# A Mamba-2 scan and a SiLU block on one core: the loads of unit 2 move from ScalarE's queue to GpSimd's

## The chip, the cores and the metric

The kernel runs on one core of a Trainium2 chip. The metric is the device time of one execution in microseconds (us); smaller is better. The engines of the core run beside each other, each through its own list of instructions in a fixed order, and wait for one another by semaphores: TensorE (PE: matmuls; PEld: loading of weights), VectorE (DVE), ScalarE (ACT), GpSimd (POOL) and SyncE (SP, which here only issues transfers). Sixteen DMA engines move data between HBM and the on-chip memory. SP, ScalarE and GpSimd can each issue transfers; the issue is one instruction in that engine's list.

## The reference

The first half is a state-space scan over chunks of 32 tokens, the second an MLP with SiLU. Sizes: batch 4, 8 heads, 768 tokens, head size 32, state size 16; 3072 tokens by 256 for the MLP, with 2048 hidden columns.

```python
log_a = np.log(np.clip(a, 1e-06, 1.0))
for c in range(nc):                       # chunks of 32
    cum = np.cumsum(la, axis=-1)
    L = np.exp(cum[:, :, :, None] - cum[:, :, None, :]) * causal
    M = np.einsum('bhin,bhjn->bhij', Cc, Bc) * L
    y = np.einsum('bhij,bhjd->bhid', M, xc) + np.einsum('bhin,bhnd->bhid', Cc, state) * np.exp(cum)[..., None]
    Bx = np.einsum('bhjn,bhjd->bhjnd', Bc, xc) * np.exp(cum[:, :, -1:] - cum)[..., None, None]
    state = np.exp(la.sum(-1))[..., None, None] * state + Bx.sum(axis=2)
x = y.transpose(0, 2, 1, 3).reshape(3072, 256)
h = x @ w_in                              # 256 x 2048
out = (h / (1 + np.exp(-h))) @ w_out      # 2048 x 256
```

## The kernel before

**Tiling.** The tokens are cut into 12 units of 256 tokens (three for each of the four batches), and each unit into four chunks of 64. Two units make a pair, and the MLP works on a pair (512 tokens). Units 0 and 1 and the MLP of pair 0 are written out as a start-up script (L691 to L777) and the list `steps` (L836); from then on a loop `step(s)` interleaves the MLP of one pair with the scans of the next. The order of the instructions on every engine is that of the program text; no scheduler moves anything.

**A unit's scan.** `a` is clamped to 1e-6..1. Two DVE scans (`f_Ek`, `f_E1`) make the decay matrix E from the tile `ab`, one (`f_P`) makes the prefix products `pfx` from `pz`. `f_TP` transposes B and C of a unit on TensorE (L390); ScalarE copies them out (`bh`, `ct`) and scales C (`ce`). `f_B` multiplies B by the last column of E (`BT`). `f_G` (L437) and `f_D0` (L423) are the products on TensorE, `f_S` the state (DVE, `st`), `f_SM` two scalings of it on ScalarE (`sm`, L464), `f_C` gives `cw`, `f_M` multiplies in E, `f_Y` (L477, L486) makes the output and `f_X` copies it to `xf` on ScalarE. Units 0 and 1 take `ab` from a small matmul; from unit 2 on it is loaded from scratch tensors in HBM.

**Scratch tensors.** `a_first` holds the clamped `a` of batch 0 (unit 2 reads it). `a_in` (with a zero ahead of every chunk) and `a_zero` (first column zero) hold that of batches 1 to 3, from unit 3 on. They are made so: `f_A1` loads `a` into the tile `acl` (three loads on SP, L267), `f_A2` clamps it on DVE (L273) and writes it out by two transfers on SP (L274, L275); `f_A0` writes the zero columns from GpSimd's queue (L283). `load_ab(3)` and `load_pa(3)` read them back.

**Weights.** They come as 64-bit numbers in 16 tiles `raw` of 512 KB (0 to 7 of `w_in`, 8 to 15 of `w_out`), all loaded on SP. For each, `w_size` runs two ScalarE operations (L188, L191), `w_bits` three on DVE (L202 to L205) and one or two on GpSimd (L207), and the fp32 tile w is ready. In the start-up, `f_s1(u, j)` (L526, eight matmuls) multiplies unit u's `xf` by weight tile j, with a SiLU on ScalarE after it (`gT`, L529); `f_s2` (L539) is the second matrix. `raw` has six buffers (pool `quad`).

**Loads of the first units.** ScalarE's queue issues B of unit 0 (L248), C of unit 2 (L743) and B of unit 2 (L752), each as two transfers of 64 KB in pieces of 64 bytes. GpSimd's queue issues B and C of unit 1, half of x of unit 1, x of unit 2 and B of unit 3, SP's all else. In the compiled program every transfer that SP or ScalarE issues takes one of eight completion semaphores, and its issue waits until the earlier transfer with that semaphore has landed. GpSimd's have eight of their own.

The script around the change, before (cut):

```python
    f_Ek(1, 0)
    load_n(2, 1, nc.scalar)
    ...
    f_s1(0, 2)
    w_bits(3, 2)
    w_size(4)
    f_A0()
    load_n(2, 0, nc.scalar)
    ...
    f_SM(1)
```

Of the kernel before, what the change touches and what calls it, by code (L numbers as in the profile page):

```python
# [8 lines left out]
FP32 = mybir.dt.float32  # L9
# [4 lines left out]
ALU = mybir.AluOpType  # L14
# [19 lines left out]
def kernel(  # L34
# [22 lines left out]
    nc = tc.nc  # L57

    batch, H, S, D = x.shape
    N = B.shape[-1]  # L60
    Q = 64
# [9 lines left out]
    loads = ctx.enter_context(tc.tile_pool(name="loads", bufs=1))  # L71
# [14 lines left out]
    def block(name, dtype=FP32):  # L86

        return blk.tile([128, 512], dtype, name=name, tag="blk", bufs=NB)
# [20 lines left out]
    def load_ab(u, q):  # L109
        ab[u] = loads.tile([128, 2, H, Q], FP32, name="ab")  # L110
        src, n = (a_first, 4 * u) if u < UPB else (a_zero, 4 * u - NC0)
        for c in range(2):
            q.dma_start(out=ab[u][64 * c:64 * c + 64].rearrange("p k h t -> p k (h t)"),
                        in_=src[n + c:n + 4:2].rearrange("(o k) h t -> o k (h t)", o=1).to_broadcast([64, 2, H * Q]))

    def load_n(u, i, q):
        b, t0 = at(u)
        if i == 0:
            t = bn[u] = (block("bn0")[:, 0:256].rearrange("p (k h n) -> p k h n", k=2, h=H) if u in (0, 1, 3) else
                         loads.tile([128, 2, H, N], FP32, name="bn"))  # L120
        else:
            t = tbc[u] = block("tbc0")[:, 0:256].rearrange("p (k h n) -> p k h n", k=2, h=H)
        for k in range(2):
            q.dma_start(out=t[:, k], in_=(B, C)[i][b, :, t0 + 128 * k:t0 + 128 * k + 128].rearrange("h p n -> p h n"))

    def load_t(u, i, q):
        b, t0 = at(u)
# [16 lines left out]
    def load_bcx(u, what="bcx"):  # L144
        if "c" in what:
            if 0 < u < UPB:
                load_n(u, 1, nc.sync)
            else:
                load_t(u, 0, nc.sync)
                load_t(u, 1, nc.sync)  # L150
        if "b" in what:
            load_n(u, 0, nc.sync)
        if "x" in what:
            load_x(u, nc.sync)
# [19 lines left out]
    def load_w(n, q):  # L174
        j = n % 8
        src = wi[:, :, j * WF:(j + 1) * WF] if n < 8 else wo[:, 2 * j:2 * j + 2]
        if src.dtype == FP32:
            w32[n] = block("w32")
            q.dma_start(out=two(w32[n]), in_=src)
            return  # L180
        t = raw[n] = quad.tile([128, 2, WF, 2], U32, name="raw", tag="quad")
        q.dma_start(out=t.rearrange("p k f two -> p k (f two)"), in_=src.bitcast(U32))

    def w_size(n, what="uv"):
        if n in raw:
            if "u" in what:
                u = wu[n] = block("wu")
                nc.scalar.activation(two(u), raw[n][:, :, :, 1].bitcast(FP32), AF.Abs)  # L188
            if "v" in what:
                v = wv[n] = block("wv")  # L190
                nc.scalar.activation(two(v), raw[n][:, :, :, 0], AF.Copy, scale=2.0 ** -51, bias=2.0)  # L191

    def w_bits(n, parts=1):
        if n in raw:
            u, v, hi = two(wu.pop(n)), two(wv.pop(n)).bitcast(U32), raw[n][:, :, :, 1]
            w32[n] = block("w32")
            for i in range(parts):
                fs = slice(WF // parts * i, WF // parts * (i + 1))
                if i == 0 or n == 0:
                    ws = fs if n == 0 else slice(0, WF)  # L200
                    ui = u[:, :, ws].bitcast(U32)
                    nc.vector.tensor_scalar(out=u[:, :, ws], in0=u[:, :, ws], scalar1=LEAST, scalar2=MOST,  # L202
                                            op0=ALU.max, op1=ALU.min)
                    nc.vector.tensor_scalar(out=ui, in0=ui, scalar1=3, scalar2=None, op0=ALU.logical_shift_left)
                    nc.vector.scalar_tensor_tensor(out=v[:, :, ws], in0=hi[:, :, ws], scalar=0x80000000, in1=v[:, :, ws],  # L205
                                                   op0=ALU.bitwise_and, op1=ALU.bitwise_or)
                nc.gpsimd.tensor_tensor(out=two(w32[n])[:, :, fs].bitcast(U32), in0=u[:, :, fs].bitcast(U32),  # L207
                                        in1=v[:, :, fs], op=ALU.add)
# [23 lines left out]
    NC1 = NC0 * (batch - 1)  # L232
# [34 lines left out]
            nc.sync.dma_start(out=acl[NC0 * (b - 1):NC0 * b],  # L267
                              in_=bass.AP(tensor=a.tensor, offset=a.offset + b * H * S, ap=[[Q, NC0], [S, H], [1, Q]]))

    def f_A2():  # L270

        r = slice(0, NC1)
        nc.vector.tensor_scalar(out=acl[r], in0=acl[r], scalar1=1.0, scalar2=1e-6, op0=ALU.min, op1=ALU.max)  # L273
        nc.sync.dma_start(out=a_in[:, :, 1:].rearrange("h c t -> c h t"), in_=acl[r])  # L274
        nc.sync.dma_start(out=a_zero[:, :, 1:], in_=acl[r, :, 1:])  # L275

    misc = block("misc")
    idle = misc[:, 0:UT].bitcast(BF16)
    nc.vector.memset(idle, 0.0)

    def f_A0():
        for t in (a_in[:, :, 0:1].rearrange("h c t -> c h t"), a_zero[:, :, 0:1]):
            nc.gpsimd.dma_start(out=t, in_=misc[:NC1, 0:H].rearrange("p (h t) -> p h t", t=1))  # L283

    warm = nc.const_aps.tensor(1.0, [128, 512], BF16)

# [50 lines left out]
    def f_P0(u, engine):  # L337
        src = pa[u].rearrange("p (c t) -> p c t", t=Q)
        PZ[u] = (pz, pz1, pz)[u]
        engine.tensor_scalar(out=PZ[u][:, :, 1:], in0=src, scalar1=1.0, scalar2=1e-6, op0=ALU.min, op1=ALU.max)  # L340
# [32 lines left out]
    def f_B(u, engine=nc.vector, ks=slice(0, 2)):  # L373
        if u not in BT:
            BT[u] = sc.tile([128, 2, H, N], FP32, name="BT")
        engine.tensor_tensor(out=BT[u][:, ks], in0=bn[u][:, ks],
                             in1=E[u][:, ks, :, Q - 1:Q].to_broadcast([128, ks.stop - ks.start, H, N]), op=ALU.mult)
# [144 lines left out]
    def f_s1(u, j):  # L522
        hp = two(half("hp"))
        for i in range(2):
            for kc in range(KC):
                nc.tensor.matmul(out=hp[:, i], lhsT=two(w32[j])[:, kc, 128 * i:128 * i + 128],  # L526
                                 rhs=two(XF[u])[:, kc], start=(kc == 0), stop=(kc == KC - 1))
        GT[u, j] = block("gT")
        nc.scalar.activation(two(GT[u, j]), hp, AF.Silu)  # L529
        if j == 7:  # L530
            XF.pop(u)
# [169 lines left out]
    f_A1()  # L701
    load_a(2)
    load_w(4, nc.sync)
    load_ab(2, nc.sync)
    load_w(5, nc.sync)
    f_Ab(0, 1, slice(4, 8))
    f_Ek(0, 0, slice(4, 8))
    f_Ek(0, 1, slice(0, 4))
# [22 lines left out]
    busy(2)  # L731
    f_X(0)
    w_bits(1, 2)
    w_size(2)
    f_s1(0, 0)
    w_size(3)
    w_bits(2, 2)
    f_s1(0, 1)
    f_TP(1)
    for e in range(2):  # L740
        f_T2(1, e)
    f_Ek(1, 0)
    load_n(2, 1, nc.scalar)  # L743
    for n in range(6, 8):
        load_w(n, nc.sync)
    f_Ek(1, 1)
    f_B(1, nc.gpsimd)
    f_s1(0, 2)
    w_bits(3, 2)
    w_size(4)  # L750
    f_A0()
    load_n(2, 0, nc.scalar)  # L752
    for n in range(8, 10):
        load_w(n, nc.sync)
    load_bcx(3, "c")
    f_G(1)
    f_D0(1)
    w_bits(4, 2)
    f_P(1)
    f_C(1, nc.gpsimd)  # L760
    f_P0(2, nc.gpsimd)
    load_x(2, nc.gpsimd)
    f_S(1)
    f_SM(1)
    f_M(1, 0)
# [5 lines left out]
    f_X(1)  # L771
    w_size(6)
    w_bits(5)
    f_A2()
    load_pa(3, nc.sync)
    load_w(10, nc.sync)
    load_n(3, 0, nc.gpsimd)  # L777

    def stage(u, what):
        for c in what:  # L780
            if c == "L":
                load_unit(u)
            elif c == "a":
                load_ab(u + 1, nc.sync)
            elif c == "x":
                load_x(u, nc.sync)
            elif c == "T":
                if 0 < u < UPB:
                    f_TP(u)
                else:  # L790
                    f_T(u, 0)
                    f_T(u, 1)
                f_T2(u, 0)
                f_T2(u, 1)
            elif c == "P":
                f_P(u)
            elif c in "12":
                f_E1(u, int(c) - 1, 2)
            elif c == "B":
                f_B(u)  # L800
            elif c == "C":
                f_C(u)
            elif c == "D":
                f_G(u)
                f_D0(u)
            elif c == "M":
                f_M(u, 0)
                f_M(u, 1)
            elif c == "S":
                f_S(u)  # L810
            elif c == "s":
                f_SM(u)
            elif c == "Y":
                f_Y(u)
                f_X(u)
            elif c == "h":
                f_xh(u)
            elif c == "l":
                f_xl(u)
            elif c == "d":  # L820
                f_xd(u)
# [4 lines left out]
    def todo(text):  # L826

        for step in text.split():
            if ":" in step:
# [3 lines left out]
            n = int(step[1:].split(".")[0])  # L833
            {"b": w_bits, "s": w_size, "h": w_h, "l": w_l, "d": w_d, "v": partial(w_d, vector=True), "m": f_s2, "p": s1_d, "r": load_r}[step[0]](n)

    steps = ((1, 0, "2:PT1"), (1, 1, "2:C2Ba"), (1, 2, "3:x b6 r11 s7"), (1, 3, "2:DSsM r12"),  # L836
             (1, 4, "b7 r13 s8"), (0, 5, "3:T s9"), (1, 5, "2:Y b8 r14"), (0, 6, "3:1PC s10"),
             (1, 6, "b9 r15 3:2B s11 h0 l0"), (0, 7, "2:h s12"), (1, 7, "3:D b10 3:SsM"))
    for u, j, text in steps:
# [119 lines left out]
```

## Time and profile before

| | us |
|---|---|
| median of 3 runs | 339.09 (338.19 to 339.94) |
| the profiled execution | 338.53 |
| its span, first to last instruction | 336.8 |
| TensorE busy | 323.6 (96%) |
| VectorE busy | 249.3 (74%) |
| ScalarE busy | 220.8 (66%) |
| GpSimd busy | 87.8 (26%) |

Mean granted TensorE clock: 0.989. The busy times are of one execution, taken by the hardware profiler. Waiting and the issuing of transfers are not counted as busy. In the page's slices each digit is the busy share of a fortieth of the span, in tenths. In a chain of waits each line is a piece of work or waiting that the next one needed.

### The profile page before, as it was taken

The numbers are of one execution on the slowest core, as the hardware profiler recorded it, in microseconds if no ns is written. First come the engines' busy times: TensorE is split into PE (matmuls) and PEld (weight loads), VectorE is DVE, ScalarE is ACT, GpSimd is POOL, SyncE is SP. The second block draws the span as 40 slices with busy tenths as digits, with TensorE's granted clock in tenths as the row PEclk, the third lists the DMA queues.
The fourth block names the chain that finished last, engine by engine and source line by source line (L and its number), as shares of the span: only waits on it lengthen the run. The fifth ranks groups of instructions, "written<-read, shape, count | busy, mean of one in ns | idle before, by whom it ended". The sixth has DMA issues, their size and how long they took to land.

```text
span 336.8 us, 7981 instructions
## 1 busy us (share of the span) xinstructions
PE 323.6 (96%) x3219; PEld 262.1 (78%) x3221; DVE 249.3 (74%) x414; ACT 220.8 (66%) x422; POOL 87.8 (26%) x89
## 2 busy tenths in 40 slices
PE   8883999999999999999999999999999999999995
PEld 5552788888878778878778778788778788899995
DVE  7964579987778798998866897965996873484443
ACT  3652568676568998857685766676666756656661
POOL 6865524557310212122102231202231202000000
PEclk9999699999999999999999999999999999999999
DMA  6999475777876394263340164420153000012001
GB/s 136 284 271 271 120 199 172 183 129 137 160 141 109 83 170 83 55 115 64 77 84 0 47 111 71 110 45 0 49 110 64 2 2 0 0 25 40 0 2 62
DMA packets 85732, 31.87 MB, mean 95 GB/s; under 512 B 69364, under 2 KB 76276, under 8 KB 85696
## 3 DMA queue, kind: packets, MB, share of 16 engines
q1 hardware_dynamic: 75888, 24.68, 31.9%
q0 software_dynamic: 3280, 6.03, 9.7%
q10 hardware_dynamic: 6528, 0.66, 1.5%
q8 instruction: 25, 0.41, 0.5%
q14 instruction: 11, 0.09, 0.1%
HBM read 22.79 MB, written 3.32 MB: 78 GB/s over the span
## 4 chain that ended last, share of the span: by engine, by line
PE 90%; DVE 4%; DMA 3%; issue 1%; ACT 0%; DVEq 0%
PE hp L562 23%; PE hp L554 11%; PE oa L603 9%; PE oa L604 9%; PE b L634 9%; PE oa L539 8%; PE hp L526 6%; PE gy L486 3%; PE b L629 2%; PE b L612 2%; PE oa L612 2%; PE gy L477 2%; DMA raw<-in_moe_w_in_dram 2%; PE gy L437 2%; PE gy L423 1%; DVE E L352 1%
## 5 line engine op out<-in xcount | busy, mean ns | idle before, releaser
L556 ACT ACTIVATE hp<-hp 128x512 f32<-128x512 f32 x80 | 46.6, 582 | 70.6 <-PE hp L554 70.5
L576 DVE TENSOR_TENSOR gl<-g,gh 128x512 fp32r<-128x512 f32 x62 | 42.8, 690 | 50.4 <-ACT gh L572 47.5
L562 PE MATMUL hp<-xh,wh 128*128 128x512 f32 x160 | 65.4, 409 | 0.0
L580 DVE SCALAR_TENSOR_TENSOR gd<-gh,g 128x512 fp32r<-128x512 f32 x80 | 59.5, 747 | 5.2 <-ACT gh L572 5.2
L562 PE MATMUL hp<-xl,wl 128*128 128x512 f32 x160 | 62.7, 392 | 0.0
L576 POOL TENSOR_TENSOR gl<-g,gh 128x512 fp32r<-128x512 f32 x18 | 29.3, 1629 | 121.5 <-ACT gh L572 121.5
L572 ACT ACTIVATE gh<-g 128x512 fp32r<-128x512 f32 x80 | 50.6, 632 | 2.7
L603 PE MATMUL oa<-gh,wh 128*128 128x512 f32 x128 | 50.0, 390 | 0.0
L604 PE MATMUL oa<-gl,wl 128*128 128x512 f32 x128 | 49.9, 390 | 0.0
L554 PE MATMUL hp<-xd,wd 128*128 128x512 f32 x160 | 49.6, 391 | 0.0
L570 ACT ACTIVATE g<-hp 128x512 f32<-128x512 f32 x80 | 47.5, 594 | 0.6 <-PE hp L562 0.6
L562 PEld LDWEIGHTS hp<-xh,wh 128*128 128x128 f32 x160 | 30.1, 188 | 8.8 <-ACT hp L556 2.6
L526 PE MATMUL hp<-xf,w 128*128 128x256 f32 x128 | 31.9, 402 | 4.5 <-POOL w L207 3.9
L554 PEld LDWEIGHTS hp<-xd,wd 128*128 128x128 f32 x160 | 30.0, 188 | 6.6
L634 PE MATMUL b<-gd,wd 128*128 128x512 f32 x128 | 34.5, 389 | 0.0
L562 PEld LDWEIGHTS hp<-xl,wl 128*128 128x128 f32 x160 | 30.1, 188 | 4.8
L207 POOL TENSOR_TENSOR w<-wu,wv 128x512 uint32<-128x512 uint32 (+1 forms) x21 | 26.1, 1250 | 25.3 <-DVE wv L205 25.3
L526 PEld LDWEIGHTS hp<-xf,w 128*128 128x128 f32 x128 | 24.5, 199 | 10.0 <-POOL w L207 5.8
L352 DVE TENSOR_TENSOR_SCAN E<-ab,diag 128x512 f32<-128x512 f32 (+1 forms) x26 | 29.1, 1150 | 1.3 <-PE ab L359 0.8
L539 PE MATMUL oa<-gT,w 128*128 128x256 f32 x128 | 28.8, 381 | 0.0
L603 PEld LDWEIGHTS oa<-gh,wh 128*128 128x128 f32 x128 | 24.0, 188 | 5.1
L604 PEld LDWEIGHTS oa<-gl,wl 128*128 128x128 f32 x128 | 24.0, 188 | 5.1
(105 smaller groups left out, 468.2 us busy)
## 6 DMA issues: line engine op xcount, KB each, us to landing
ab<-a_zero SPq DMA_DIRECT2D x18, 256.0 KB
raw<-in_moe_w_in_dram SPq DMA_DIRECT2D x8, 512.0 KB
raw<-in_moe_w_out_dram SPq DMA_DIRECT2D x8, 512.0 KB
wl<-w POOLq DMA_DIRECT2D x16, 256.0 KB, 4.0
xt<-in_x_dram SPq DMA_DIRECT2D x21, 128.0 KB
out_dram<-ot SPq DMA_DIRECT2D x40, 64.0 KB
tbc<-in_C_dram SPq DMA_DIRECT2D x40, 32.0 KB
pz<-a_in SPq DMA_DIRECT2D x9, 130.0 KB
```

The source lines that it names most:

```text
L526: nc.tensor.matmul(out=hp[:, i], lhsT=two(w32[j])[:, kc, 128 * i:128 * i + 128], rhs=two(XF[u])[:, kc], start=(kc == 0), stop=(kc == KC - 1))
L539: nc.tensor.matmul(out=OA[0][m][:, UT * u:UT * u + UT], lhsT=two(w32[8 + j])[:, i, 128 * m:128 * m + 128], rhs=two(GT[u, j])[:, i], start= ...
L554: nc.tensor.matmul(out=HP[s], lhsT=two(WD[f // 2])[:, kc, 128 * (f % 2):128 * (f % 2) + 128], rhs=XD[P][:, kc], start=(kc == 0), stop=Fals ...
L556: nc.scalar.activation(HP[s], HP[s], AF.Copy, scale=HALF / UP)
L562: nc.tensor.matmul(out=HP[s], lhsT=two(w[f // 2])[:, kc, 128 * (f % 2):128 * (f % 2) + 128], rhs=x_[P][:, kc], start=False, stop=(kc == KC ...
L570: nc.scalar.activation(G[s], HP.pop(s), AF.Silu, scale=UP)
L572: nc.scalar.activation(GH[s], G[s], AF.Copy, scale=DOWN)
L576: engine.tensor_tensor(out=GL[s], in0=G[s], in1=GH[s].bitcast(FP32), op=ALU.subtract)
L580: nc.vector.scalar_tensor_tensor(out=GD[s], in0=GH[s].bitcast(FP32), scalar=1.0 + 1.0 / HALF, in1=G.pop(s), op0=ALU.mult, op1=ALU.subtract)
L603: nc.tensor.matmul(out=OA[P][m], lhsT=two(WH[n])[:, r, ms], rhs=gh, start=(f == 0), stop=False)
L604: nc.tensor.matmul(out=OA[P][m], lhsT=two(WL[n])[:, r, ms], rhs=gl, start=False, stop=(f == NF - 1))
L634: nc.tensor.matmul(out=B2[P][:, m], lhsT=two(WD[n])[:, r, 128 * m:128 * m + 128], rhs=gd, start=(fresh and s == tiles[0]), stop=True, skip ...
```

## The change

ScalarE issues only B of unit 0 (two transfers). C of unit 2 goes to GpSimd's queue in two halves, with w3 between them, B of unit 2 and x of unit 3 as whole loads. The clamp of `acl` moves from DVE to GpSimd and is done twice: in place, after w1 (`f_A2(True)`), and once more into a block of its own `acz`, with its first column set to zero, after w2 (`f_A2(False)`). The writes to the scratch tensors become `f_A3`, three transfers on SP right after raw tile 7: the zero column of `a_in`, `a_in`, and all of `a_zero`. On SP, raw 5 goes ahead of `ab` of unit 2; C and B of unit 3 and `pz` of unit 3 ahead of raw 8 and 9; raw 10 behind `ab` of unit 3.

```diff
-    def load_n(u, i, q):
+    def load_n(u, i, q, ks=(0, 1)):
         b, t0 = at(u)
-        if i == 0:
-            t = bn[u] = (block("bn0")[:, 0:256].rearrange("p (k h n) -> p k h n", k=2, h=H) if u in (0, 1, 3) else
-                         loads.tile([128, 2, H, N], FP32, name="bn"))
-        else:
-            t = tbc[u] = block("tbc0")[:, 0:256].rearrange("p (k h n) -> p k h n", k=2, h=H)
-        for k in range(2):
-            q.dma_start(out=t[:, k], in_=(B, C)[i][b, :, t0 + 128 * k:t0 + 128 * k + 128].rearrange("h p n -> p h n"))
+        if i == 1:
+            if u not in tbc:
+                tbc[u] = block("tbc0")[:, 0:256].rearrange("p (k h n) -> p k h n", k=2, h=H)
+        elif u not in bn:
+            bn[u] = (block("bn0")[:, 0:256].rearrange("p (k h n) -> p k h n", k=2, h=H) if u in (0, 1, 3) else
+                     loads.tile([128, 2, H, N], FP32, name="bn"))
+        for k in ks:
+            q.dma_start(out=(bn, tbc)[i][u][:, k], in_=(B, C)[i][b, :, t0 + 128 * k:t0 + 128 * k + 128].rearrange("h p n -> p h n"))
...
-    def f_A2():
+    acz = block("acz").rearrange("p (h t) -> p h t", t=Q)
+
+    def f_A2(first):
 
         r = slice(0, NC1)
-        nc.vector.tensor_scalar(out=acl[r], in0=acl[r], scalar1=1.0, scalar2=1e-6, op0=ALU.min, op1=ALU.max)
+        nc.gpsimd.tensor_scalar(out=(acl if first else acz)[r], in0=acl[r], scalar1=1.0, scalar2=1e-6, op0=ALU.min, op1=ALU.max)
+        if not first:
+            nc.gpsimd.memset(acz[r, :, 0:1], 0.0)
+
+    def f_A3():
+
+        r = slice(0, NC1)
+        nc.sync.dma_start(out=a_in[:, :, 0:1].rearrange("h c t -> c h t"), in_=misc[r, 0:H].rearrange("p (h t) -> p h t", t=1))
         nc.sync.dma_start(out=a_in[:, :, 1:].rearrange("h c t -> c h t"), in_=acl[r])
-        nc.sync.dma_start(out=a_zero[:, :, 1:], in_=acl[r, :, 1:])
+        nc.sync.dma_start(out=a_zero, in_=acz[r])
...
-    def f_A0():
-        for t in (a_in[:, :, 0:1].rearrange("h c t -> c h t"), a_zero[:, :, 0:1]):
-            nc.gpsimd.dma_start(out=t, in_=misc[:NC1, 0:H].rearrange("p (h t) -> p h t", t=1))
...
     load_w(4, nc.sync)
+    load_w(5, nc.sync)
     load_ab(2, nc.sync)
-    load_w(5, nc.sync)
...
     w_bits(1, 2)
+    f_A2(True)
     w_size(2)
     f_s1(0, 0)
     w_size(3)
     w_bits(2, 2)
+    f_A2(False)
     f_s1(0, 1)
     f_TP(1)
     for e in range(2):
         f_T2(1, e)
     f_Ek(1, 0)
-    load_n(2, 1, nc.scalar)
     for n in range(6, 8):
         load_w(n, nc.sync)
     f_Ek(1, 1)
     f_B(1, nc.gpsimd)
+    load_n(2, 1, nc.gpsimd, (0,))
     f_s1(0, 2)
     w_bits(3, 2)
     w_size(4)
-    f_A0()
-    load_n(2, 0, nc.scalar)
-    for n in range(8, 10):
-        load_w(n, nc.sync)
-    load_bcx(3, "c")
+    load_n(2, 1, nc.gpsimd, (1,))
+    f_A3()
     f_G(1)
     f_D0(1)
     w_bits(4, 2)
     f_P(1)
     f_C(1, nc.gpsimd)
     f_P0(2, nc.gpsimd)
+    load_n(2, 0, nc.gpsimd)
     load_x(2, nc.gpsimd)
+    load_bcx(3, "c")
+    load_pa(3, nc.sync)
     f_S(1)
     f_SM(1)
...
     w_bits(5)
-    f_A2()
-    load_pa(3, nc.sync)
-    load_w(10, nc.sync)
+    for n in range(8, 10):
+        load_w(n, nc.sync)
     load_n(3, 0, nc.gpsimd)
...
             elif c == "x":
-                load_x(u, nc.sync)
+                load_x(u, nc.gpsimd)
...
-    steps = ((1, 0, "2:PT1"), (1, 1, "2:C2Ba"), (1, 2, "3:x b6 r11 s7"), (1, 3, "2:DSsM r12"),
+    steps = ((1, 0, "2:PT1"), (1, 1, "2:C2Ba r10"), (1, 2, "3:x b6 r11 s7"), (1, 3, "2:DSsM r12"),
```

## The prediction

> **What bounds the kernel now.** I read the page's slices first, then the chain of waits in order of time, then the engines' timelines and a table of stretches around the place that the chain pointed to.
>
> ```profile
> PE   8883999999999999999999999999999999999995
> PEclk9999699999999999999999999999999999999999
> DMA  6999475777876394263340164420153000012001
> ```
>
> One slice is 8.42 us. From slice 5 on (33.7 us) TensorE is busy all the time, at full clock from slice 6 on: a wait on another engine after about 40 us costs nothing, and whatever brings TensorE to that point earlier should move the end by the same amount. The only hole is slice 4 (25 to 34 us, busy 3 tenths), and slice 5 is the only one with a low clock. Here is the chain of waits across it (start, length, what):
>
> ```profile
> 21.34 6.79 DMA raw<-in_moe_w_in_dram
> 28.13 0.02 issue
> 28.16 3.59 DMA bn<-in_B_dram
> 31.74 0.02 issue
> 31.77 0.70 ACT sm L464 x2
> ...
> 32.56 1.08 PE gy L477 x32
> 33.64 1.13 PE gy L486 x61
> ...
> 35.23 3.78 PE hp L526 x8
> 39.01 0.75 PE gy L390 x4
> 39.75 5.18 PE hp L526 x24
> ```
>
> A 128-column scaling on ScalarE (sm) waits for a load that it does not read. The timeline of ScalarE says why:
>
> ```profile
> 20.47 2.37 ACTq L124 DMA_DIRECT2D tbc<-in_C_dram  x2
> 22.88 0.60 ACT L529 ACTIVATE gT<-hp 128x512 f32<-128x512 f32 x1 [2.34 <-DMA ab<-a_first]
> 28.16 3.56 ACTq L124 DMA_DIRECT2D bn<-in_B_dram  x2
> 31.77 0.69 ACT L464 ACTIVATE sm<-st,par 128x128 f32<-128x128 f32 x2 [7.17 <-DMA bn<-in_B_dram]
> ```
>
> ScalarE issues C and B of unit 2 itself. One issue takes 0.375 us (the view of L124), but in the compiled order each waits until an older transfer on the same completion semaphore has landed: B's first for raw tile 7 (28.13), its second for a later one. So ScalarE stands for 2.34 and 7.17 us. DVE had written st by 27.50 (its row at 26.27 lasts 1.23), so sm could have run then. TensorE meanwhile:
>
> ```profile
> 28.70:32.50 3.80, 0.03 (x1) 0.00 (x0) 0.00 (x0) 0.73 (x3) 1.73 (x2) 1.00 1.06 240
> 32.50:34.80 2.30, 2.19 (x96) 1.86 (x96) 1.24 (x3) 2.07 (x5) 0.00 (x0) 0.54 0.48 80
> 36.00:39.50 3.50, 3.50 (x12) 2.77 (x11) 1.07 (x1) 1.01 (x2) 3.50 (x3) 0.50 0.36 74
> ```
>
> Columns: stretch, length, busy PE, PEld, DVE, ACT, POOL, clock, DMA share, GB/s. After 3.8 us without matmuls the clock is half for about 7 us. The gap costs twice: 3.8 us of waiting, and about 7 x 0.5 = 3.4 us of slow matmuls.
>
> **What the Trainium skill says.** "DMA: Bandwidth & Descriptors", section Anatomy of one DMA: the DMA engines do not wait on semaphores, the wait is on the issuing sequencer before dispatch. The trace agrees: two issues of 0.375 us hold ScalarE for 3.56. The same page, Issuing engines are not separate DMA queues: loads from any engine run on the same 16 DMA engines, so moving the issue saves only the issuer's time. The DMA share of 1.06 at 28.7 to 32.5 fits: no bandwidth is gained. "TensorE: Matmul & The Clock Gate", section What's actually happening: one idle window of about 3.4 us halves the clock; the 3.8 us gap agrees. "GPSIMD Engine Reference", Specifications: GpSimd shares SBUF interfaces with VectorE; L207 on 128x512 took 3.03 us at 35.10 against 1.26 at 44.43, which fits.
>
> **The change part by part**, as a re-timing of 15 to 40 us on the times of this trace. Names: w3 is weight tile 3; s1(u,j), G, D0, Y, TP are TensorE's blocks of unit u.
>
> *GpSimd gains two clamps and a memset.* In the new order A2(True) stands between w1 and w2 on GpSimd, and it waits for the three loads of acl. They were issued at 12.61 to 14.06 on SP right behind a_first, and a_first landed just before 17.80, when SP's load of ab that waits for it goes. I take 18.5 for acl. GpSimd's rows now:
>
> ```profile
> 17.75 1.42 POOL L207 TENSOR_TENSOR w<-wu,wv 128x256 uint32<-128x256 uint32 x2 [0.63 <-DVE wv L205]
> 20.05 0.68 POOL L376 TENSOR_TENSOR BT<-bn,E 128x256 f32<-128x256 f32 x1 [0.89 <-issue]
> 21.69 1.41 POOL L207 TENSOR_TENSOR w<-wu,wv 128x256 uint32<-128x256 uint32 x2 [0.96 <-DVE wv L205]
> 25.64 1.72 POOL L207 TENSOR_TENSOR w<-wu,wv 128x256 uint32<-128x256 uint32 x2 [0.92 <-DVE wv L205]
> ```
>
> A clamp of 256 columns costs 0.39 (L340), and L207 goes from 0.71 to 1.26 when its columns double, so a clamp of 512 is about 0.7. The queue: clamp 18.55 to 19.25; w2 (1.42) to 20.7, so 1.5 later; second clamp and memset to 21.6; BT 22.3 (was 20.73); first half of C(2), 0.92 as the loads of GpSimd show, to 23.3; w3 to 24.7 (was 23.1); second half of C(2) to 25.6; w4 to 27.1 (was 27.36); cw 0.7 and the clamp of pz 0.4 to 28.2; B(2), two issues, 28.25 to 30.1; x(2) to 32. Bounds of a clamp: 0.4 and, if it is stretched like the slow L207 (x 2.4), 1.7.
>
> *ScalarE loses four issues.* TensorE starts s1(0,2) on the first half of w2 at 20.1 and ends at 22.05 (was 20.5). So gT is at 22.1, the two halves of w_size(4) at 22.6 and 23.2: 0.77 earlier than now, although 2.34 of waiting went; the delay of w2 eats the rest. DVE: w4's bits to 24.8 (was 25.55), pfx 0.7, st 1.2, ending 26.7; M to 27.95. sm follows st at 26.7 to 27.4, against 31.77.
>
> *TensorE.* G and D0 of unit 1 at 22.1 to 23.2, s1(0,3) 24.0 to 26.0 (was 22.47), s1(0,4) 26.4 to 28.4, then Y(1): sm, M and cw are all there, so it starts at 28.4 instead of 32.56. At full clock it takes 1.4 (as in the later Y rows, 0.62 + 0.79), xf 0.45: s1(1,0) runs 30.3 to 32.1, where it ended at 39.01. Up to here 6.9 us are gained, and no gap of TensorE is longer than about 1.3 us, so the low clock should not come.
>
> *What is late next: B(2).* TP(2) is the next block, and it reads it. Now B(2) was in long before 39.01; in the new order its second issue starts on GpSimd at 29.2. GpSimd's loads of B took 4.3 (issued at 38 to 40, queue nearly empty) and 7.8 (issued at 6 to 9, queue full) from issue to landing; x(2), issued at 28.55, took 4.0. In the new order raw 8 and 9 stand behind unit 3's B, C and pz on SP, so the load is light there; I take 4.3. B(2) lands at 33.5, three transposes more: TP(2) ends at 33.95 instead of 39.75, of which TensorE idles 1.4. Gain: 5.8 us.
>
> *The rest*, at nothing. C(2) is issued at 22.35 and 24.7 and even at 7.8 us lands at 32.5, before B(2). raw 8 and 9 land some 3 us later, at about 34; ScalarE reads raw 8 at 48.37 now, about 42.5 then. raw 10 moves from 38.05 to behind ab(3), which waits for DVE's second scan (42.52 now, 37.1 then), and its raw tile is read after 55 now. x(3) from GpSimd adds 1.9 us of issue ahead of w6; GpSimd is free from 33.3, w6's input comes from DVE at 38.5, and TensorE needs w6 only after Y(2). If this cover were gone, w6 would be late by at most these 1.9 us. DVE's clamp (0.41 at 34.93) was no wait. The write of a's zero column goes from GpSimd to SP, which has nothing urgent then. pz(3) is earlier than before. After 40 us the order of the other engines hangs on TP(2), since DVE's cw waits 3.87 for ScalarE's ce behind it, so they move up with it.
>
> Sum: the profiled execution took 338.53 (span 336.8 and 1.7 around it); minus 5.8 is 332.7. The median shown is 339.09, 0.56 above. I forecast 333.0.
>
> **The rivals.**
> *GpSimd becomes the bound.* For: two clamps, a wait and eight more issues in its queue, and L207 at 3.03 us once. Against: it is busy 7.22 of the 10 us from 10 to 20 and 3.71 of the next 5, so 4 of 15 us are free. Clamps of 1.7 put w4, cw and B(2) 2.0 later: TP(2) at 35.95, gain 3.8; with acl another 1 us later 2.8. About 335.2.
> *The new wait replaces the old one.* B(2) is late and TensorE idles so long that the clock drops again. With a landing at about 35.5 the gap from 32.1 is 3.4, the loss of clock 3.4, and TensorE is at 35.95 + 3.4 = 39.35 where it is 39.75 now: about 338.4, no change. For: 7.1 to 7.8 us for GpSimd's 64 KB loads when queues were full (1.06 DMA share at 28.7). Against: 4.0 for x(2) in that very stretch.
> *Slower: the same load, as slow as the slowest here.* GpSimd 1 us late, so issued at 30.2, 7.8 to land: 38.0, TP(2) to 38.45, a gap of 5.9 and 3.4 of half clock: 41.85 against 39.75, 2.1 lost, 340.6. It decides from a landing at 35.9 on (35.9 + 0.45 + 3.4 = 39.75), 6.7 us after an issue at 29.2.
>
> **How the numbers follow.** Forecast 333.0: 0.66, its own range 331.3 (B(2) not late at all: TP(2) would end at 32.55, gain 7.2) to 334.8. GpSimd bound: 0.14. Wait replaced: 0.08. Slower: 0.12. The range reaches into the second case: 331.3 to 336.8. Half a per cent is 1.7 us, about what a measurement of this kernel tells from no change. Faster 0.80 (the first two), same 0.08, slower 0.12.
>
> **What would show it.** In the new profile: no ACTq row after the first two; sm at about 27; w2 on GpSimd at about 19.3 behind the clamp; Y(1) at about 28.4 and slice 5 of PEclk at full; a PE wait for B(2) of 1 to 2 us before L396 and s1(1,1) at about 34. The forecast is wrong if that wait is over 3 us or brings a half clock, if acl lands well after 18.5, or if TensorE shows new holes after 40 us, with raw 8 to 10 or w6 as the releaser.

## The result and the profile after

The median of 20 runs is 335.96 us (333.86 to 340.54), that of the kernel before, 20 runs beside them, 339.90 (338.19 to 340.98). The ratio is 0.9882, 95% interval 0.9857 to 0.9908: the change saves 3.9 us of the 6.1 that were forecast (333.0 against 339.09). The ratio is that of the means without the runs more than 1.5% above a kernel's fastest (five of these twenty, 338.93 to 340.54 us, and two each in x2_later and three_raws below); with all twenty it is 0.9912. The other fifteen still spread from 333.86 to 338.48, where the kernel before spreads over 2.8 us. They sort by TensorE's mean clock: seven with 0.998 or more lie at 333.86 to 336.00, seven with 0.993 to 0.995 at 334.86 to 338.48, one with 0.988 at 338.17; the five left out have 0.990 to 0.995, no less than these. (Half clock for 3.4 us, as in the profiled execution, takes 0.005 off the mean: 0.5 x 3.4 / 336.7.) The profiled execution took 338.48 us, the slowest of the fifteen, and so shows what goes wrong. The page's slices:

```profile
PE   8868699999999999999999999999999999999996
PEclk9999799999999999999999999999999999999999
DMA  6997685777886394263440163430163000012001
```

The hole of slice 4 is filled, from 3 to 8 tenths. But slice 3 fell from 8 to 6, slice 5 from 9 to 6, and slice 5 kept a low clock (7 tenths, before 6). TensorE's timeline (start, length, line, out<-in, shapes, count, idle time ahead and what ended it; the lines of the changed kernel that are quoted here are numbered 1 to 6 higher from L116 on):

```profile
29.59 0.69 PE L483 MATMUL gy<-cw,sm 32*64 32x64 f32 x32
...
31.55 1.99 PE L532 MATMUL hp<-xf,w 128*128 128x256 f32 x8 [0.47 <-ACT xf L502]
33.97 0.30 PE L396 MATMUL gy<-ident,bn 128*128 128x128 f32 x1 [0.43 <-DMA bn<-in_B_dram]
37.30 0.33 PE L396 MATMUL gy<-ident,bn 128*128 128x128 f32 x1 [3.03 <-DMA bn<-in_B_dram]
...
37.82 6.89 PE L532 MATMUL hp<-xf,w 128*128 128x256 f32 x24
```

Y(1) starts at 29.59 instead of 32.56 and s1(1,0) ends at 33.5 instead of 39.0. Then TP(2) waits 0.43 us for the first half of B of unit 2 and 3.03 for the second. The chain of waits runs through the same place:

```profile
28.85 0.40 POOL pz L346
29.25 0.06 issue
29.31 0.94 POOL bn L125
30.25 0.00 issue
30.25 7.00 DMA bn<-in_B_dram
37.26 0.04 issue
37.30 0.73 PE gy L396 x3
38.03 6.68 PE hp L532 x24
44.71 0.62 PE gy L443 x32
```

GpSimd has issued the second half at 30.25, and it lands 7.00 us later. The 24 matmuls after it take 6.68 us; at full clock they take 5.3 (5.38 for the next 24). The table of stretches (stretch, length, busy PE, PEld, DVE, ACT, POOL, clock, DMA share, GB/s) shows the gap and the clock after it:

```profile
34.00:37.20 3.20, 0.27 (x1) 0.08 (x1) 1.27 (x1) 0.17 (x1) 3.20 (x5) 1.00 1.05 305
37.50:40.90 3.40, 3.40 (x11) 2.77 (x10) 1.65 (x3) 1.11 (x3) 0.13 (x1) 0.50 0.43 84
```

By 44.71 this execution is only 0.23 us ahead of the kernel before (44.94), and it ends as early as that one (338.48 against 338.53). The gain of 3.9 us is presumably that of executions in which this second gap costs less; none of them was profiled.

What went out beside B? SP's timeline and GpSimd's, in this order:

```profile
29.30 0.62 SPq L106 DMA_DIRECT2D pz<-a_in  x1
30.02 0.93 SPq L183 DMA_DIRECT2D raw<-in_moe_w_out_dram  x2
```

```profile
18.97 0.61 POOL L276 TENSOR_SCALAR acl<-acl 36x512 f32<-36x512 f32 x1 [1.03 <-DMA acl<-in_a_dram]
19.66 1.41 POOL L208 TENSOR_TENSOR w<-wu,wv 128x256 uint32<-128x256 uint32 x2
...
29.31 1.83 POOL L125 DMA_DIRECT2D bn<-in_B_dram  x2
31.13 1.76 POOL L143 DMA_DIRECT2D xt<-in_x_dram  x2
```

SP issued raw 8 and 9, 1 MB, 0.2 us before the second half of B, and x of unit 2 stood right behind it on GpSimd. Either could be what held it up. The clamp waited 1.03 us for acl, and w2 behind it.

### The profile page after: what moved, and what is told of

It reads as the page before. It is cut to its first block, busy times and chain, and to the rows that moved or that the text cites. A ratio compares the mean times of both kernels' runs of the same rounds, so it can differ in the third digit from the quotient of the medians.

```text
span 336.7 us, 7984 instructions
## 1 busy us (share of the span) xinstructions
PE 324.1 (96%) x3219; PEld 261.5 (78%) x3221; DVE 253.2 (75%) x413; ACT 221.1 (66%) x422; POOL 91.6 (27%) x96
## 4 chain that ended last, share of the span: by engine, by line
PE 90%; DMA 8%; POOL 1%; SPq 0%; DVE 0%; issue 0%
PE hp L568 23%; PE hp L560 11%; PE oa L609 9%; PE oa L610 9%; PE b L640 9%; PE oa L545 8%; PE hp L532 6%; DMA a_first<-ach 3%; PE gy L492 2%; PE b L635 2%; PE b L618 2%; PE oa L618 2%; PE gy L443 2%; DMA bn<-in_B_dram 2%; DMA ab<-a_first 2%; PE gy L483 2%
## 5 line engine op out<-in xcount | busy, mean ns | idle before, releaser
L582 POOL TENSOR_TENSOR gl<-g,gh 128x512 fp32r<-128x512 f32 x18 | 29.2, 1621 | 121.9 <-ACT gh L578 121.9
L358 DVE TENSOR_TENSOR_SCAN E<-ab,diag 128x512 f32<-128x512 f32 (+1 forms) x26 | 30.9, 1213 | 1.7 <-PE ab L365 1.1
L208 POOL TENSOR_TENSOR w<-wu,wv 128x512 uint32<-128x512 uint32 (+1 forms) x21 | 24.1, 1153 | 21.4 <-DVE wv L206 21.2
```

Source lines behind the costliest of these rows:

```text
L582: engine.tensor_tensor(out=GL[s], in0=G[s], in1=GH[s].bitcast(FP32), op=ALU.subtract)
```

## The experiments

All times are medians; each set of runs has the kernel before beside it on its chip (339.39, 340.06, 340.46 and 340.13 us). The table gives the ratio to it. Each run has one profiled execution, and what is read from it holds for that execution.

| run | what differs | median (lowest to highest) us | ratio to before, 95% |
|---|---|---|---|
| the change | | 335.96 (333.86 to 340.54) | 0.9882, 0.9857 to 0.9908 |
| raw89_later | raw 8, 9 behind ab(3) | 334.44 (333.63 to 335.27) | 0.9847, 0.9823 to 0.9872 |
| x2_later | x(2) behind B(3) | 336.33 (332.72 to 340.05) | 0.9860, 0.9819 to 0.9902 |
| b2_on_sp | B(2) issued by SP | 334.13 (332.42 to 334.85) | 0.9831, 0.9806 to 0.9855 |
| filled_gap | matmuls on zeros ahead of TP(2) | 336.21 (335.02 to 338.15) | 0.9910, 0.9879 to 0.9941 |
| scalar_issues | C(2), B(2) on ScalarE again | 336.55 (334.89 to 338.25) | 0.9891, 0.9854 to 0.9928 |
| only_queue | before, C(2) and B(2) on GpSimd | 333.89 (333.09 to 334.32) | 0.9809, 0.9776 to 0.9841 |
| clamp_after_w2 | first clamp behind w2 | 333.81 (333.30 to 336.21) | 0.9824, 0.9789 to 0.9859 |
| all_three | loads on SP, clamps late, raw 8, 9 late | 333.68 (332.59 to 334.97) | 0.9803, 0.9771 to 0.9835 |
| three_raws | raw 10 with raw 8, 9 | 337.40 (334.74 to 341.64) | 0.9877, 0.9822 to 0.9932 |
| sp_loads_late_clamp | all_three with raw 8, 9 ahead of unit 3 | 332.25 (331.99 to 333.02) | 0.9769, 0.9734 to 0.9804 |
| old_order_sp_loads | before, C(2) and B(2) on SP | 332.88 (332.06 to 333.75) | 0.9780, 0.9744 to 0.9817 |
| raw89_sooner | raw 8, 9 ahead of C(3) | 336.69 (334.64 to 339.33) | 0.9899, 0.9871 to 0.9927 |

### Why is B of unit 2 late?

**raw89_later.**

```diff
-    for n in range(8, 10):
-        load_w(n, nc.sync)
...
-    steps = (... (1, 1, "2:C2Ba r10"), ...
+    steps = (... (1, 1, "2:C2Ba r8 r9 r10"), ...
```

> After, with the loads of raw tiles 8 and 9 moved on SP behind ab of unit 3. Theory (the second half of B(2), issued at 30.25, landed only at 37.26 because SP issued these 1 MB at 30.02 to 30.95, and the two share the DMA engines): both halves of B(2) land about 4.5 us after their issue, so by 34.8; TensorE's wait before TP(2) falls from 3.0 to about 0.8 us, its clock stays full, s1(1,1) starts at about 35.3 and the runs lie near 334.5, within about 1 us of each other. Rival 1 (GpSimd's own loads behind it, x(2) at 31.1 to 32.9, hold it up): the landing stays near 37 and the times as in the changed kernel, 334 to 340. Rival 2 (pieces of 64 bytes just vary): likewise no shift of the median, 336.

TensorE's timeline at TP(2):

```profile
35.40 0.72 PE L396 MATMUL gy<-ident,bn 128*128 128x128 f32 x2 [0.95 <-DMA bn<-in_B_dram]
35.95 0.38 PE L396 MATMUL gy<-ident,tbc 128*128 128x128 f32 x2
36.17 5.34 PE L532 MATMUL hp<-xf,w 128*128 128x256 f32 x24
```

The second half of B was issued at 31.16 and landed 4.6 us later; the wait is 0.95 instead of 3.03 and the clock behind it full (5.34 for 24 matmuls). The four runs lie within 1.6 us. Their interval (0.9823 to 0.9872) still overlaps that of the change, so it is the profile more than the time that speaks here. s1(1,1) starts 0.9 us later than I expected, because acl came later in this execution (GpSimd waited 2.72 for it, and TensorE's clock was at half from 22 on: 0.57 over the stretch from 22 to 26).

**x2_later**, the rival's test.

```diff
-    load_x(2, nc.gpsimd)
     load_bcx(3, "c")
...
     load_n(3, 0, nc.gpsimd)
+    load_x(2, nc.gpsimd)
```

> After, with x of unit 2 issued on GpSimd behind w5 and B of unit 3 instead of right behind B(2). Theory (raw 8 and 9 hold up B(2)): the second half still lands at about 36 to 37, times as in the changed kernel, median about 336. Rival 1 (x(2) on the same queue holds it up): the second half lands by 35, the wait before TP(2) is under 1 us, median about 334.5.

TensorE at TP(2), and SP:

```profile
36.67 0.33 PE L396 MATMUL gy<-ident,bn 128*128 128x128 f32 x1 [2.27 <-DMA bn<-in_B_dram]
...
37.05 7.03 PE L532 MATMUL hp<-xf,w 128*128 128x256 f32 x24
```

```profile
30.71 0.91 SPq L183 DMA_DIRECT2D raw<-in_moe_w_out_dram  x2
```

With no transfer behind B(2) on GpSimd's queue until 34.05, the second half, issued at 30.70, still took 5.9 us, and raw 8 was issued at 30.71. The median and the spread (332.72 to 340.05) are those of the changed kernel. What follows behind B on its queue is not the main cause; whether it makes the difference between 5.9 and 7.0 us was not separated.

**three_raws**, more of the suspected bytes.

```diff
-    for n in range(8, 10):
+    for n in range(8, 11):
         load_w(n, nc.sync)
...
-    steps = (... (1, 1, "2:C2Ba r10"), ...
+    steps = (... (1, 1, "2:C2Ba"), ...
```

> After, with raw 10 loaded right behind raw 8 and 9 as well, so 1.5 MB instead of 1 MB stand on SP at the moment when GpSimd issues B(2). Theory (B(2) is late by the bytes that SP has put in flight beside it): where SP's raw 8 comes first, the second half of B(2) lands 1 to 1.7 us later than the 37.3 of the changed kernel, the gap brings the half clock more often, median 337 to 339. Rival (the lateness has nothing to do with the raw tiles): median 336, as the changed kernel.

The runs fall apart into two groups: 334.74, 335.16 and 335.23 with a clock of 1.0, and 339.57, 339.86 and 341.64 with 0.983 to 0.990. The profiled one is of the first group; its SP, and TensorE at TP(2):

```profile
31.61 1.69 SPq L183 DMA_DIRECT2D raw<-in_moe_w_out_dram  x3
```

```profile
34.16 0.30 PE L396 MATMUL gy<-ident,bn 128*128 128x128 f32 x1
34.94 0.33 PE L396 MATMUL gy<-ident,bn 128*128 128x128 f32 x1 [0.48 <-DMA bn<-in_B_dram]
```

Here raw 8 went out 0.8 us behind the second half of B, and B took 4.1 us. So the profile does not put the theory to the test, and the times do not bear it out: the group at clock 1.0 lies where the changed kernel's runs at 1.0 lie (334.47 to 335.57), the other two at 0.990 where its runs at 0.990 do (339.74 to 340.54), and the ratio, 0.9877, is that of the change. The median, 337.40, stands between the two groups of three. Whether more bytes delay B more stays open.

**raw89_sooner**, both well apart in the other order.

```diff
+    load_t(3, 0, nc.sync)
+    for n in range(8, 10):
+        load_w(n, nc.sync)
+    load_t(3, 1, nc.sync)
-    load_bcx(3, "c")
     load_pa(3, nc.sync)
...
-    for n in range(8, 10):
-        load_w(n, nc.sync)
```

> After, with raw 8 and 9 issued on SP between B and C of unit 3, so about 2 us sooner, at 27.5 to 29. Theory (what hurts is that SP's 1 MB and GpSimd's second half of B(2) start within about 1 us of each other, and either order well apart is good): the raw tiles are nearly through when the second half is issued at about 30.3, it lands by 35, no half clock there, median 334 to 335.5, runs within 2 us of each other. Rival (any 1 MB ahead of B(2) delays it by its own 3 to 4 us): B(2) is late in every run, 338 to 340.

This expectation failed, and so did the rival's "late in every run": the median is 336.69, the runs spread over 4.7 us, and two of the eleven, at 334.64 and 335.89, have a clock of 1.0. In the profile raw 8 and 9 go out from 27.84, and both halves of B, issued at 29.13 and 30.07, take 6.2 and 6.8 us:

```profile
35.46 0.30 PE L396 MATMUL gy<-ident,bn 128*128 128x128 f32 x1 [2.09 <-DMA bn<-in_B_dram]
36.95 0.47 PE L396 MATMUL gy<-ident,bn 128*128 128x128 f32 x1 [1.19 <-DMA bn<-in_B_dram]
```

So it need not be a near collision: 1 MB issued up to 2.2 us ahead is enough. The profiles together, by how far the issue of raw 8 lies from that of the second half of B (issue to landing of that half from the view of DMA issues):

| profile | issue of raw 8 | second half of B issued | raw 8 relative to it | to landing, us |
|---|---|---|---|---|
| raw89_sooner | 27.84 | 30.07 | 2.2 ahead | 6.8 |
| the change | 30.02 | 30.25 | 0.2 ahead | 7.0 |
| x2_later | 30.71 | 30.70 | together | 5.9 |
| clamp_after_w2 | 30.82 | 30.28 | 0.5 behind | 3.6 |
| three_raws | 31.61 | 30.8 | 0.8 behind | 4.1 |
| filled_gap | 31.59 | 30.43 | 1.2 behind | 3.4 |
| raw89_later | behind ab(3), from 40.44 | 31.16 | 9 behind | 4.6 |

The order goes with the time: 5.9 to 7.0 us where raw 8 is ahead or level, 3.4 to 4.6 where it is behind. The first halves fit: 3.9 to 4.5 us where they were issued 0.7 to 2.1 us ahead of raw 8 (the change, x2_later, clamp_after_w2, three_raws, filled_gap), 5.0 in raw89_later, but 6.2 in raw89_sooner and 6.7 in only_queue, where raw 8 had gone out 1.3 and 3.0 us earlier. Up to these issues x2_later, three_raws and filled_gap have the program of the changed kernel, so they count as more executions of it, and the order does differ among the four: raw 8 is 0.2 ahead, level, 0.8 behind, 1.2 behind. The two issues are on different engines and depend on different waits: GpSimd's follows its own arithmetic, SP's the landing of the transfers ahead of it.

**filled_gap**, the clock alone.

```diff
                 if 0 < u < UPB:
+                    busy(12, 0, new_dp(u)[:, 0])
                     f_TP(u)
```

> After, with 12 matmuls of 128x512 bf16 on a tile of zeros ahead of TP(2), into a bank that is overwritten later; they run while TensorE would wait for B(2). Theory (the spread of the changed kernel from 334 to 340 is the clock, which drops in some executions because of the gap at TP(2)): no stretch at half clock after 10 us, all runs within about 1.5 us, near 335. Rival (the spread is that of the landing): the spread stays at 4 us or more with the clock at full.

Neither side. The spread falls from 6.7 (twenty runs) to 3.1 us (six), but two of six runs still show a clock of 0.993 and 0.995, and the median is no better: the 12 matmuls take 2.6 us, and in the profiled execution B had landed at 33.8 while TP(2) started behind them at 36.16. This filler of fixed length saved nothing in the median (336.21).

**b2_on_sp**, B early by another way.

```diff
-    load_n(2, 0, nc.gpsimd)
     load_x(2, nc.gpsimd)
+    load_n(2, 0, nc.sync)
     load_bcx(3, "c")
```

> After, with B of unit 2 issued by SP ahead of B, C and pz of unit 3 instead of by GpSimd. Theory (the landing of B(2) is all that TensorE still waits for): B(2) lands before 31, no wait at TP(2), s1(1,1) starts at about 34.1 (33.5, the end of s1(1,0), and 0.5 for the transposes), full clock throughout, and all runs lie at 332.5 to 334. Rival (something else is late right behind B(2): C(2), the second scan, w5 or x(2)): TensorE waits there instead, the median stays at 335 to 336.

No wait before L396 (35.07 follows on s1(1,0)), and no low clock behind it; 334.13, with runs within 2.4 us. That is most of the expected gain, but s1(1,1) starts at 35.51 and not at 34.1: the clamp waited 2.65 us for acl, w2 ran at 20.45, TensorE waited 2.42 for w2, and its clock was low after that (0.57 over the stretch from 22 to 26).

### What the other parts of the change cost

**clamp_after_w2.**

```diff
     w_bits(1, 2)
-    f_A2(True)
...
     w_bits(2, 2)
+    f_A2(True)
     f_A2(False)
```

> After, with the first clamp of acl on GpSimd behind w2 instead of ahead of it. Theory (the wait for acl, 1.0 us in the profile of the changed kernel and up to 2.7 in others, is handed on by GpSimd's queue to w2, BT, w3, w4 and B(2)): w2 runs at about 18.5 to 20, s1(0,2) starts 1.1 to 2 us earlier, B(2) is issued about 1 us earlier and, ahead of raw 8 and 9, lands by 34; median 1 to 3 us below the changed kernel, 333 to 335. Rival (w2 has slack, and B(2) lands with raw 8 and 9 whenever it is issued): median about 336, as the changed kernel.

w2 starts at 18.55, s1(0,2) at 19.38 (20.44 before that edit). B is issued at 29.22, only 0.1 us earlier than in the changed kernel's profile: that step of the expectation failed in this pair. In the changed kernel's profile acl had come early: in the seven others with the clamp ahead of w2, GpSimd stood 1.6 to 2.7 us there, against 1.03. B is ahead of raw 8 here because raw 8 went out 0.8 us later (30.82), not because B went earlier. The median falls by the 2 us expected, though the interval (0.9789 to 0.9859) still touches that of the change; that the wait for acl is the reason is not shown.

**only_queue**, one part alone: the kernel before with four issues moved.

```diff
-    load_n(2, 1, nc.scalar)
+    load_n(2, 1, nc.gpsimd)
...
-    load_n(2, 0, nc.scalar)
+    load_n(2, 0, nc.gpsimd)
```

> The kernel before, with C and B of unit 2 issued by GpSimd at the same places of the program, and nothing else changed. Theory (only the issuer matters, the other parts cost what they gain): Y(1) starts at about 29 to 30, B(2) was issued at about 25 to 27 and lands before 33, no wait of more than 1 us at TP(2), full clock, 333 to 335. Rival (the clamps on GpSimd and SP's new order are needed for the gain): B(2), C(2) or w3 and w4 come late behind each other on GpSimd, 337 or more.

TensorE's timeline:

```profile
30.30 0.69 PE L477 MATMUL gy<-cw,sm 32*64 32x64 f32 x32
...
34.09 0.38 PE L390 MATMUL gy<-ident,bn 128*128 128x128 f32 x2
34.31 0.38 PE L390 MATMUL gy<-ident,tbc 128*128 128x128 f32 x2
34.52 5.34 PE L526 MATMUL hp<-xf,w 128*128 128x256 f32 x24
```

The theory holds: Y(1) starts at 30.30, B was issued at 25.75 and was in before TP(2) (34.09, no wait), the clock is full, s1(1,1) starts at 34.52. At 0.9809 it is below the interval of the whole change. The other parts of the change, added to this one, therefore cost about 2.5 us (0.7% of 340) net.

**scalar_issues**, the same part undone.

```diff
+    load_n(2, 1, nc.scalar)
     for n in range(6, 8):
...
     f_A3()
+    load_n(2, 0, nc.scalar)
```

Left out are the three `load_n(2, ...)` on GpSimd.

> After, with C and B of unit 2 issued by ScalarE again at the places of the kernel before; all other parts of the change stay. Theory (the gain of the change is ScalarE's freedom from waiting on earlier loads): ScalarE stands behind these issues again, sm comes at about 30 or later, TensorE idles over 3 us before Y(1) and the time goes back to 338 to 341. Rival (the gain is that of SP's order and of the clamps): the time stays near that of the changed kernel, 334 to 338.

This expectation failed in its size: 336.55, not 338 to 341. ScalarE's timeline shows that it does wait, and elsewhere:

```profile
24.82 2.65 ACTq L125 DMA_DIRECT2D tbc<-in_C_dram  x2
27.52 0.60 ACT L535 ACTIVATE gT<-hp 128x512 f32<-128x512 f32 x1 [6.32 <-PE hp L532]
...
30.50 1.01 ACTq L125 DMA_DIRECT2D bn<-in_B_dram  x2
31.84 0.70 ACT L470 ACTIVATE sm<-st,par 128x128 f32<-128x128 f32 x2 [2.63 <-DVE st L463]
```

SP's new order changes which earlier transfer each issue waits for. C(2) now keeps ScalarE until 27.47; the SiLU behind it (L535) could have run when its matmuls ended at 24.12, so it is 3.4 us late, and w4 with it. B(2) goes out in 1.0 and holds up nothing: sm waits for st. TensorE's clock is low twice on the way (0.55 over 20.7 to 24, 0.54 over 31.3 to 35). Y(1) starts only at 34.92, over 5 us behind the changed kernel, but TP(2) then waits for nothing and s1(1,1) starts at 39.15 at full clock, against 37.82 at half. So the other parts of the change alone gain about as much as the whole (0.9891 and 0.9882): in the new order, freeing ScalarE gained about what the late B cost.

### A version without either wait

**all_three**, a first try: C and B of unit 2 on SP behind raw 7, both clamps behind x(2), the scratch writes behind unit 3's loads, raw 8 and 9 behind ab(3).

```diff
-    f_A2(True)
-    f_A2(False)
-    load_n(2, 1, nc.gpsimd, (0,))
-    load_n(2, 1, nc.gpsimd, (1,))
-    f_A3()
+    load_n(2, 1, nc.sync)
+    load_n(2, 0, nc.sync)
+    load_bcx(3, "c")
...
-    load_n(2, 0, nc.gpsimd)
     load_x(2, nc.gpsimd)
-    load_bcx(3, "c")
+    f_A2(True)
+    f_A2(False)
+    f_A3()
     load_pa(3, nc.sync)
...
-    for n in range(8, 10):
-        load_w(n, nc.sync)
...
-    steps = (... (1, 1, "2:C2Ba r10"), ...
+    steps = (... (1, 1, "2:C2Ba r8 r9 r10"), ...
```

> After, with C and B of unit 2 on SP behind raw 7, the clamps of acl on GpSimd behind x of unit 2, the writes to the scratch tensors behind B and C of unit 3, and raw 8 and 9 behind ab of unit 3. Theory (GpSimd's queue ahead of w4 and the landing of B(2) are what is left): GpSimd is free for w2, w3 and w4 as they come from VectorE, Y(1) starts at 27 to 28, no wait at TP(2), s1(1,1) starts at about 32.5, 331 to 332.5. Rival (TensorE then waits for C(2) or B(2) behind raw 7 on SP, or for ab and pz of unit 3 later): 334 or more.

s1(1,1) starts at 33.02, but ScalarE and then TensorE wait later:

```profile
46.19 0.66 ACT L189 ACTIVATE wu<-raw 128x512 f32<-128x512 f32 x1 [4.29 <-DMA raw<-in_moe_w_out_dram]
```

```profile
48.03 1.97 PE L532 MATMUL hp<-xf,w 128*128 128x256 f32 x8 [1.90 <-ACT gT L535]
```

Raw 8, issued at 41.35, is now what is late. The edit that was good in raw89_later is bad 3 us earlier.

**sp_loads_late_clamp** puts `load_w(8)` and `load_w(9)` between B of unit 2 and `load_bcx(3, "c")` instead, and leaves `r10` as in the change.

> As all_three (C and B of unit 2 on SP behind raw 7, clamps of acl behind x of unit 2 on GpSimd), but with raw 8 and 9 right behind B of unit 2 and so ahead of B and C of unit 3. In all_three raw 8 was issued only at 41.35 and ScalarE waited 4.29 us for it, TensorE 2.3. Theory (that late raw 8 is the whole rest): s1(1,1) starts at about 33, no hole of TensorE after it, 331.0 to 332.5. Rival (B and C or pz of unit 3 are then late): a hole later, 333.5 or more.

TensorE's timeline:

```profile
27.85 0.69 PE L483 MATMUL gy<-cw,sm 32*64 32x64 f32 x32
...
32.35 0.33 PE L396 MATMUL gy<-ident,bn 128*128 128x128 f32 x1 [0.28 <-DMA bn<-in_B_dram]
32.52 0.38 PE L396 MATMUL gy<-ident,tbc 128*128 128x128 f32 x2
32.73 5.35 PE L532 MATMUL hp<-xf,w 128*128 128x256 f32 x24
```

All as expected: 332.25 us, 5 runs within 1.03 us, all at a clock of 0.998 or more. It is faster than both kernels (0.9769, interval 0.9734 to 0.9804).

**old_order_sp_loads** asks whether the clamps on GpSimd are needed at all: the kernel before with

```diff
-    load_n(2, 1, nc.scalar)
...
-    f_A0()
-    load_n(2, 0, nc.scalar)
+    load_n(2, 1, nc.sync)
+    load_n(2, 0, nc.sync)
...
     load_x(2, nc.gpsimd)
+    f_A0()
```

> The kernel before, with C and B of unit 2 issued by SP behind raw 7 and ahead of raw 8, and the writes of the zero columns on GpSimd moved behind x of unit 2; the clamp of acl stays on VectorE. Theory (neither ScalarE nor GpSimd needs to issue these loads, and the clamps on GpSimd are no part of the gain): GpSimd takes w2 to w4 as they come, Y(1) at about 28, B(2) lands by 32, s1(1,1) at about 33, full clock, 331 to 332.5. Rival (raw 8 and 9 late behind them, or a hole for a_in and pz of unit 3): 333.5 or more.

332.88 us, 0.4 above the expected range; s1(1,1) starts at 33.38. The ratio is 0.9780, no different from the one above by their intervals. With VectorE's clamp and the old writes, the gain is the same; the move of the clamp is no part of it.

## Why the prediction came out as it did

The direction and the place were right: TensorE gets past Y(1) earlier because ScalarE no longer stands behind its own issues, and the next thing late is B of unit 2. Step by step against the profile:

- *sm and Y(1)*: forecast about 27 and 28.4, measured 27.97 and 29.59. About 0.5 us is acl: taken at 18.5, the clamp started at 18.97. The rest is stretched work. sm follows VectorE, whose three operations for w4 took 0.65, 0.82 and 1.21 us instead of 0.43, 0.43 and 0.68. Y(1) follows s1(0,4), which waited for w4 on GpSimd; w4 ran at 26.64, right behind the second issue of C(2), and ahead of that BT had taken 1.14 instead of 0.68 and w3 1.63 instead of 1.41. VectorE and GpSimd now work at the same time there. The Trainium skill, "GPSIMD Engine Reference", Specifications, names shared SBUF interfaces with VectorE, which this agrees with, though no run isolates it; I had applied it to the clamps only, which took 0.61 and 0.67, as forecast.
- *No gap over 1.3 us before that, so no low clock*: right in this profile. In raw89_later's, with acl later, the clock did drop at 22.
- *B(2) issued at 29.2*: measured 30.25, following on the above.
- *B(2) lands 4.3 us after its issue*: this is the term that was mis-sized. The first half took 4.5, the second 7.0. I argued that raw 8 and 9 stand behind unit 3's loads on SP, and the load would be light. I never timed when SP would reach them. It did so at 30.02, 0.2 us ahead of that second half, and raw89_later, raw89_sooner and the table by order show that this goes with 7.0 instead of about 4. Issued at the forecast 29.2, the second half would have been 0.8 us ahead of raw 8, and by the table (an estimate) have taken some 4 us: GpSimd's delay of 1.05 us turned the order.
- *TP(2) ends at 33.95 with 1.4 us idle*: 38.03 with 3.46 idle, 4.1 us late: 1.05 from the later issue, 2.7 from the landing, and 0.3 for the rest.
- *Full clock behind it*: wrong in this execution. 24 matmuls took 6.68 us instead of 5.3, 1.4 us lost. The Trainium skill, "TensorE: Matmul & The Clock Gate", What's actually happening, takes one idle window of about 3.4 us for the half clock and calls the window free-running. The traces agree on the window (last section), but not on the idle time: waits of 2.27 us (x2_later), 2.31 (raw89_later) and 2.08 (scalar_issues) ahead of the matmuls brought the half clock too, while 2.75 in only_queue and 2.10 in three_raws did not. So the length of a gap alone does not decide. Whether the window's phase or B's landing decides in one execution was not separated.

4.1 and 1.4 of the 5.8 us are gone in the profiled execution. By the prediction's own signs, a wait over 3 us and a half clock, the forecast was wrong there. The time is that of the rival "the new wait replaces the old one" (338.4, measured 338.48), but through two errors that cancel. B landed at 37.26, not at 35.5, and so beyond the 35.9 from which the prediction expected a loss; issue and landing are nearer its third rival. And the half clock cost 1.4 us, not 3.4, because it lasted half as long. (Before, too, it cost less than 3.4: by the rows about 2.9, with Y(1) 2.21 for 1.41, s1(1,0) 3.78 for 1.99 and TP(2) 0.75 for 0.45.)

Over all runs the kernel lies between that rival and the forecast. The median, 335.96, is within the stated range of 331.3 to 336.8, and in part by luck: the prediction had one landing time for B and knew of no race between two queues, whose outcome now decides the time of a run.

*Costed at nothing.* Right: no hole of TensorE after 40 us in the profile, so raw 8 to 10, w6, x(3) and pz(3) stayed covered. That execution was hardly ahead of the kernel before by then; but clamp_after_w2, with s1(1,1) at 34.27, has none either. What that cover is worth shows in all_three: with raw 8 at 41.35 and TensorE 5 us earlier, 2.3 us.

Not tried: the clamps on VectorE inside the new order, and a profile of one of the changed kernel's runs at 334 us.

## What to carry to other kernels

An issue in a compute engine's list is as long as the wait in front of it (here two of 0.375 us held ScalarE for 3.56), so before moving it look up which earlier transfer it waits for, and put it where that one has long landed. A queue whose waits hold up no arithmetic (SP here) did best in these runs (0.9769 and 0.9780), as long as the loads behind it did not become late in turn. When a wait goes, work out the next load on the path as carefully as the wait itself: not only when it is issued and its usual latency, but what other queues put in flight in the few microseconds ahead of it. And a spread of times that grows, here from 2.8 to 6.7 us (2%) with the clock following it, can be the sign of a race between two queues; with both transfers on one queue, in sp_loads_late_clamp, the runs lay within 1.03 us.

## What the hardware showed that I had not expected

A 64 KB load in 64-byte pieces, issued by GpSimd, took 3.4 to 4.6 us when 1 MB from SP was issued behind it, even by only 0.5 us, and 5.9 to 7.0 when the same 1 MB was issued level with it or up to 2.2 us ahead (seven profiles, one execution each).

The half clock came in pieces of one length, or two of them in a row. Summed over stretches of 0.2 us, it lasted 3.41 to 3.42 us in the changed kernel, x2_later, raw89_later, b2_on_sp and twice in scalar_issues, and twice that, 6.82 and 6.83, in the kernel before and in raw89_sooner. In these last two TensorE stood idle again within the first 3.4 us, for 0.47 and 1.19 us; in the other six by at most 0.16. In scalar_issues the two pieces begin at 21.06 and 31.30, 10.24 us or three such lengths apart. The clock need not drop at the gap itself: in raw89_later matmuls had been running again for 1.28 us (from 21.08) when it fell at 22.36, in x2_later for 0.9.
